# Steps of attention and of the weight sums in other slots, and the sign of converted weights by a sloped ReLU

## The chip, the cores and the metric

The kernel runs on one core of one Trainium2 chip. A core has a matrix engine (TensorE, PE in the profile), a vector engine (VectorE, DVE), a scalar engine (ScalarE, ACT), GpSimd (POOL) and SyncE (SP), which here issues the transfers (DMA). Each engine takes its own instructions in order and waits where an input isn't there yet. The metric is the device time of one execution in microseconds (us).

## What is computed

Chunked attention, then a feed-forward layer with a gated activation, all in float32:

```python
scores = scale * np.matmul(q_c, k_c.transpose(0, 1, 2, 4, 3))      # q, k, v: 8 x 8 heads x 576 x 64, chunks of 64
scores = scores - np.max(scores, axis=-1, keepdims=True)
attn = np.exp(scores)
attn = attn / (np.sum(attn, axis=-1, keepdims=True) + 1e-09)
x = np.matmul(attn, v_c)                                           # reordered to 4608 tokens x 512
h = x @ w_in                                                       # 512 x 2048
g = h * np.clip(h + 3.0, 0.0, 6.0) / 6.0
out = g @ w_out                                                    # 2048 x 512
```

The two weight matrices are handed over as float64 and are converted to float32 on the core.

## The kernel before, in words

The 4608 tokens are nine blocks of 512. Every float32 product is done in three passes (`passes`, L219): each operand is split into a rounded high part and the rest, and TensorE multiplies high by high, high by low and low by high. So VectorE and ScalarE split everything that enters a product: ScalarE makes the high part, VectorE subtracts it.

**Weights.** They come as 16 tiles of 1 MB. `convert` (L100) takes the two 32-bit words of each float64 apart. ScalarE multiplies the high word, read as a float32, by 2^-112 (L106); VectorE shifts the result left by 3 bits (L107), which leaves exponent and mantissa in place and drops the sign; a VectorE instruction takes the sign bit from the high word and puts it in (L108, the mask); ScalarE scales the low word (L110), VectorE adds it (L111), and L115 and L116 split the sum into high and low.

**Blocks 0 to 2** are done directly, by slots. A slot pair is one of the 16 tiles of the hidden dimension: the even slot holds `mm1` (L225, 12 matmuls of 128x512, then ScalarE's Relu L233, VectorE's L234, ScalarE's cast L235 and, at the end of the slot, VectorE's L236, which give the two parts of `g`), the odd slot holds `mm2` (L242, another 12 matmuls, two pairs behind). A slot's 12 matmuls set its length on TensorE. There are 96 slots, in four segments of the blocks 0, 1, 0, 2.

**Blocks 3 to 8** follow in three pairs with a fast scheme of seven products in place of eight (`first_product` L498, `second_product` L558). It needs sums and differences of quarters of the weights, which are made during the slots and kept in DRAM: `prepare(m, p)` (L328) is one unit, sixteen of them. A unit stores three raw quarters (L333, three transfers), adds the two parts of two weight tiles (L337, twice), makes four sums or differences (L347), casts them to high parts in the buffer `hl` (L350, ScalarE), subtracts for the low parts (L352) and stores four quarters from `hl` (L355, four transfers). Both `a` and `hl` have one buffer each.

**Attention** of a block is done in two halves (`Attention`, L128): loads of q and k and of v by SP, scores (64 matmuls, L154), softmax in four steps (maximum L161; subtraction L164 and ScalarE's exponential L165; sum L168 and reciprocal; product L172), transposes on TensorE (L183), ScalarE's copy of them out of PSUM (L185), the matmuls with V (L194), and the copy of the result (L200, or L203 and L206). All its PSUM goes through one buffer of two banks, `two`.

**The order.** Up to slot 30 (`SUMS`) the planner of the framework orders the instructions of each engine by its own costs. From there on the order is that of the program, written out in `plan`: a table from the slot to the steps that follow that slot's own instructions, sorted by a rank. Attention's rank is the place of the step in its list, the unit steps have rank 20, so within a slot attention comes first. Attention of the halves of blocks 2 to 4 starts at slots 30, 38, 52, 60, 68 and 76 (L418), each with the offsets of `later`. The sixteen units start at slots 30, 33, 36, 40, 43, 46, 50, 53, 57, 60, 63, 67, 70, 73, 77 and 80, one step a slot. At slot 86 (`FREE`) the room of the weights and of the sums is given to the fast scheme.

Of the kernel before, what the change touches and what calls it, by code (L numbers as in the profile page):

```python
# [8 lines left out]
F32 = mybir.dt.float32  # L9
# [4 lines left out]
AF = mybir.ActivationFunctionType  # L14
ALU = mybir.AluOpType
# [15 lines left out]
NFP = NFT // 2  # L31
# [10 lines left out]
def tile_kernel(ctx: ExitStack, tc: tile.TileContext, qk_in, v_in, weights, out):  # L42
    nc = tc.nc
    PE, ACT, DVE, POOL = nc.tensor, nc.scalar, nc.vector, nc.gpsimd
# [44 lines left out]
    words, w, w_h, w_l = {}, {}, {}, {}  # L89
# [10 lines left out]
    def convert(ft):  # L100

        u = wsc.tile([P, 1024], I32, name="u")
        r = wsc.tile([P, 1024], I32, name="r")
        lo, hi = words[ft][:, :, 0], words[ft][:, :, 1]

        ACT.activation(out=u.bitcast(F32), in_=hi.bitcast(F32), func=AF.Copy, scale=2.0 ** -112)  # L106
        DVE.tensor_scalar(out=u, in0=u, scalar1=3, scalar2=None, op0=ALU.logical_shift_left)  # L107
        DVE.scalar_tensor_tensor(out=u, in0=hi, scalar=-2 ** 31, in1=u, op0=ALU.bitwise_and, op1=ALU.bitwise_or)  # L108

        ACT.activation(out=r, in_=lo.bitcast(U32), func=AF.Copy, scale=2.0 ** -29)  # L110
        DVE.tensor_tensor(out=u, in0=u, in1=r, op=ALU.add)  # L111
        a = u.bitcast(F32).rearrange("p (m t) -> p m t", m=2)
        w[ft] = w_tile(ft, F32R)
        w_h[ft], w_l[ft] = w[ft][:, 0], w[ft][:, 1]
        ACT.copy(out=w_h[ft], in_=a)  # L115
        DVE.tensor_tensor(out=w_l[ft], in0=a, in1=w_h[ft].bitcast(F32), op=ALU.subtract)  # L116

    def convert_to(ft):
        nonlocal converted
        load_to(ft + 3)  # L120
        while converted < min(ft, NFT):
            convert(converted)
            converted += 1
# [91 lines left out]
    def finish():  # L215
        while low:
            low.pop(0)()
# [56 lines left out]
    def moe_slots(n, ft, *seg):  # L274

        g = mm1(n, ft)
        yield
        pending.append((n, ft, g, *seg))
        if len(pending) > LAG:
            mm2(*pending.pop(0))  # L280
        yield
# [35 lines left out]
    def kept(m, p, i):  # L317

        if m:
            return stream_b[i, p // 4][:, p % 4]  # L320
        k = ORDER_A.index(i)
        return stream_a[p, k // 4][:, k % 4]

    def quarter(m, row, col):

        return (col, row) if m else (row, col)

    def prepare(m, p):  # L328
        cols = lambda k: slice(256 * k, 256 * k + 256)
        for i, row, col in ((1, 0, 0), (2, 0, 1), (4, 1, 1)):  # L330
            f, k = quarter(m, row, col)
            to = kept(m, p, i).rearrange("p (l t) -> p l t", l=2)
            nc.sync.dma_start(out=to, in_=w[p + NFP * f][:, :, m, cols(k)].bitcast(F32))  # L333
        a = sp.tile([P, 2, 512], F32, name="a")
        for f in range(2):
            h, l = [w[p + NFP * f][:, k, m].bitcast(F32) for k in range(2)]
            DVE.tensor_tensor(out=a[:, f], in0=h, in1=l, op=ALU.add)  # L337
        yield

        def q(row, col):  # L340
            f, k = quarter(m, row, col)
            return a[:, f, cols(k)]


        for to, x, y, op in ((q(1, 1), q(1, 0), q(1, 1), ALU.add), (q(1, 0), q(0, 0), q(1, 0), ALU.subtract),
                             (q(0, 0), q(1, 1), q(0, 0), ALU.subtract), (q(0, 1), q(0, 1), q(0, 0), ALU.subtract)):
            DVE.tensor_tensor(out=to, in0=x, in1=y, op=op)  # L347
        hl = sp.tile([P, 2, 2, 2, 256], F32R, name="hl")
        s = a.rearrange("p f (k t) -> p f k t", k=2)
        ACT.copy(out=hl[:, :, :, 0], in_=s)  # L350
        yield
        DVE.tensor_tensor(out=hl[:, :, :, 1], in0=s, in1=hl[:, :, :, 0].bitcast(F32), op=ALU.subtract)  # L352
        for i, row, col in ((5, 1, 1), (7, 1, 0), (6, 0, 0), (3, 0, 1)):
            f, k = quarter(m, row, col)
            nc.sync.dma_start(out=kept(m, p, i), in_=hl[:, f, k].rearrange("p l t -> p (l t)").bitcast(F32))  # L355
        yield


# [4 lines left out]
    def fetch():  # L363
        if stream:
            t, n = stream.pop(0)
            w = wsp.tile([P, 4, 2, 256], F32R, name="ws")
            nc.sync.dma_start(out=w[:, :n].rearrange("p n l t -> p (n l t)").bitcast(F32), in_=t[:, :n].rearrange("p n t -> p (n t)"))
            ahead.append(w)
# [11 lines left out]
    def x_operands(s, eng):  # L380

        n = NSTD + 2 * s
        b = [[xraw[n + j][:, i] for j in range(2)] for i in range(NDP)]
        sub = lambda out, x, y: eng.tensor_tensor(out=out, in0=x, in1=y, op=ALU.subtract)
        ops[s] = {}
        sub(b[0][1], b[0][1], b[0][0])
        for i in ORDER_A:
            ops[s][i] = operand()
            r, c = WHERE[i]
            split(ops[s][i], b[r][c])  # L390

            if i == 5:
                sub(b[0][1], b[1][1], b[0][1])
            elif i == 6:
                sub(b[0][0], b[0][1], b[0][0])
                sub(b[0][1], b[1][0], b[0][1])
            yield
# [3 lines left out]

    plan = {}
    early = [(0, "load_qk"), (1, "load_v"), (2, "scores"), (2, "softmax"), (7, "transpose"), (10, "values")]
    later = [(-2, "load_qk"), (3, "load_v"), (3, "scores"), (4, "soft", 0), (4, "soft", 1), (5, "soft", 2), (5, "soft", 3),
             (8, "transpose"), (9, "values")]

    def put(n, dp, at, steps, stretch=1.0):
        a = Attention(n, dp)
# [7 lines left out]
    SUMS = first[1] + 22  # L416
    FREE = first[3] + 2 * (NFP + LAG + 1)
    for (n, dp), at in zip(((2, 0), (2, 1), (3, 0), (4, 0), (4, 1), (3, 1)), (30, 38, 52, 60, 68, 76)):  # L418
        put(n, dp, at, later)
    for u in range(2 * NFP):  # L420
        for k in range(3):
            plan.setdefault(SUMS + u * (FREE - 2 - SUMS) // (2 * NFP) + k, []).append((20, lambda: next(prep)))
    prep = (step for p in range(NFP) for m in range(2) for step in prepare(m, p))
    slot = 0
    sp = made = None
    order = ExitStack()

    for i, (n, lo, hi) in enumerate(SEGMENTS):
        last = all(m != n for m, *_ in SEGMENTS[i + 1:])
        for ft in range(lo, hi):  # L430
            if i == 0:
                convert_to(min(ft + 2, 4))
            elif slot < SUMS:

                with tc.issue_after(second.done.ins):
                    convert_to(5)
                with tc.issue_after(second.last.ins):
                    convert_to(min(6 + 2 * ft, NFT))
            elif slot == SUMS:
                scratch.close()  # L440
                sums = ExitStack()
                sp = sums.enter_context(tc.tile_pool(name="sp", bufs=1, side="right"))
                op = sums.enter_context(tc.tile_pool(name="op", bufs=4, side="right"))
                order.enter_context(tc.manual_schedule())
            for _ in moe_slots(n, ft, ft == lo, ft == hi - 1, not last):
                for _, f in sorted(plan.pop(slot, []), key=lambda s: s[0]):
                    f()
                finish()
                slot += 1
                if slot == FREE:  # L450
                    assert next(prep, None) is None
                    sums.close()
                    op = None
                    start.close()
                    upper.close()
                    xop_pool = pool("xop", 8, side="right")
                    wsp = pool("wsp", 3, side="right")
                    for _ in range(3):
                        fetch()
                    made = x_operands(0, DVE)  # L460
                elif slot > FREE:
                    next(made, None)
# [197 lines left out]
```

## Time and profile before

| what | value |
|---|---|
| median of 3 runs | 855.14 us (854.91 to 855.72) |
| the profiled execution | 855.06 us |
| its span, first to last instruction | 853.1 us |
| instructions | 13690 |
| transfers | 172.86 MB, mean 203 GB/s |
| mean granted TensorE clock | 0.982 |

The profile is one execution, taken by the hardware. Its page gives each engine's busy time; the views asked of the trace give the groups of instructions by line of the kernel, the waits (who waited for whom, in total, how often, and the longest), the timeline (start, duration, engine, line, operation, tile written and tiles read, and in brackets the idle time of the engine before it and what ended it), and windows (busy time of every engine in a stretch, with the clock that TensorE was granted as a share of full speed). Engines PE and PEld are the matmuls and the weight loads of TensorE; the latter overlap the former, and matmuls overlap one another, so durations of single matmuls don't add up. The stretch from the first matmul of block 0 to about 127 us is ordered by the planner; from 127 to 321 us run the slots 30 to 85; the fast scheme fills the rest.

### The profile page before, as it was taken

What the parts mean: (1) busy time and instruction counts of PE and PEld (TensorE: products, weight loads), DVE (VectorE), ACT (ScalarE), POOL (GpSimd) and SP (SyncE); (2) the same over time, 40 slices, a digit from 0 to 9 for tenths busy, and PEclk for the clock granted to TensorE, in tenths of its full rate; (3) what the DMA queues carried; (4) which work ended last, traced back from release to release, by engine and by line L of the source; (5) the groups of instructions that cost most, each with busy time, mean ns of one, the idle gap of its engine ahead of it and who ended that gap; (6) DMA issues with size and microseconds to landing.
All of it is one profiled execution on the core that took longest, in us unless ns stands there. A gap on an engine that the chain in (4) does not pass through costs nothing.

```text
span 853.1 us, 13690 instructions
## 1 busy us (share of the span) xinstructions
PE 814.5 (95%) x5683; PEld 658.7 (77%) x5683; DVE 635.8 (75%) x768; ACT 369.1 (43%) x455; POOL 132.0 (15%) x77
## 2 busy tenths in 40 slices
PE   7889999789998999999999999999999999999998
PEld 5766878568776777878878888788788887887886
DVE  5978997585866776487699946876899466669951
ACT  4747763243334334334455443344554333336330
POOL 0000000000001000022227002222370022326200
PEclk9898999899999999999999999999999999999999
DMA  9893003856768745166655576666554765555563
GB/s 365 315 360 120 13 0 112 247 184 214 220 187 296 237 160 196 60 232 226 244 189 191 229 254 228 233 214 245 204 192 167 234 226 178 207 186 197 197 212 134
DMA packets 50014, 172.86 MB, mean 203 GB/s; under 512 B 4640, under 2 KB 16928, under 8 KB 39200
## 3 DMA queue, kind: packets, MB, share of 16 engines
q1 hardware_dynamic: 49952, 171.99, 58.0%
q8 instruction: 45, 0.74, 0.3%
q14 instruction: 17, 0.14, 0.1%
HBM read 133.17 MB, written 38.80 MB: 202 GB/s over the span
## 4 chain that ended last, share of the span: by engine, by line
PE 67%; DVE 22%; ACT 5%; issue 3%; DMA 2%; POOL 0%; SPq 0%; ACTq 0%; DVEq 0%
PE acc L221 14%; PE acc L223 14%; PE acc L222 14%; PE h L221 7%; PE h L222 7%; PE h L223 7%; PE two L194 2%; DVE xop L373 2%; DVE m L161 2%; DVE r L234 2%; DVE z L168 1%; DMA w<-w_in_out 1%; DVE a L347 1%; DVE e L164 1%; DVE g L496 1%
## 5 line engine op out<-in xcount | busy, mean ns | idle before, releaser
L221 PE MATMUL acc<-xop,ws 128*128 128x512 f32 x528 | 208.6, 396 | 4.4 <-DVE u L484 4.4
L222 PE MATMUL acc<-xop,ws 128*128 128x512 f32 x528 | 205.8, 390 | 0.0
L223 PE MATMUL acc<-xop,ws 128*128 128x512 f32 x528 | 205.4, 390 | 0.0
L221 PEld LDWEIGHTS acc<-xop,ws 128*128 128x128 f32 x528 | 99.1, 188 | 27.6 <-DVE u L484 6.8
L373 DVE TENSOR_TENSOR xop<-g,xop 128x1024 fp32r<-128x1024 f32 x72 | 103.4, 1468 | 21.5 <-ACT xop L372 21.5
L223 PEld LDWEIGHTS acc<-xop,ws 128*128 128x128 f32 x528 | 99.1, 188 | 20.9
L222 PEld LDWEIGHTS acc<-xop,ws 128*128 128x128 f32 x528 | 99.2, 188 | 19.8
L372 ACT CAST xop<-g 128x1024 fp32r<-128x1024 f32 x72 | 74.4, 1051 | 78.9 <-PE acc L223 51.3
L504 POOL TENSOR_TENSOR g<-g 128x512 f32<-128x512 f32 x24 | 34.8, 1449 | 307.3 <-DVE g L496 307.3
L221 PE MATMUL h<-x,w 128*128 128x512 f32 x192 | 80.0, 419 | 2.1 <-ACT x L203 1.2
L222 PE MATMUL h<-x,w 128*128 128x512 f32 x192 | 78.4, 409 | 0.0
L223 PE MATMUL h<-x,w 128*128 128x512 f32 x192 | 77.8, 405 | 0.0
L222 PE MATMUL acc<-g,w 128*128 128x512 f32 x192 | 75.5, 393 | 0.3 <-DVE g L236 0.3
L221 PE MATMUL acc<-g,w 128*128 128x512 f32 x192 | 75.4, 397 | 0.1
L223 PE MATMUL acc<-g,w 128*128 128x512 f32 x192 | 75.4, 393 | 0.0
L234 DVE SCALAR_TENSOR_TENSOR r<-r,h 128x512 f32<-128x512 f32 x48 | 32.8, 683 | 50.7 <-ACT r L233 50.7
L495 ACT ACTIVATE r<-acc,half 128x512 f32<-128x512 f32 x72 | 48.5, 685 | 26.3 <-DVE acc L484 25.4
L495 ACT ACTIVATE r<-h,half 128x512 f32<-128x512 f32 x24 | 16.5, 687 | 95.0 <-DVE h L484 95.0
L222 PE MATMUL h<-xop,ws 128*128 128x512 f32 x144 | 56.2, 390 | 0.2 <-DVE xop L373 0.2
L221 PE MATMUL h<-xop,ws 128*128 128x512 f32 x144 | 56.3, 391 | 0.0
L223 PE MATMUL h<-xop,ws 128*128 128x512 f32 x144 | 56.1, 389 | 0.0
L496 DVE SCALAR_TENSOR_TENSOR g<-r,acc 128x512 f32<-128x512 f32 x72 | 48.6, 683 | 7.0 <-ACT r L495 6.7
(93 smaller groups left out, 1270.5 us busy)
## 6 DMA issues: line engine op xcount, KB each, us to landing
ws<-b SPq DMA_DIRECT2D x42, 1024.0 KB, 4.8
ws<-a SPq DMA_DIRECT2D x24, 1024.0 KB, 4.9
ws<-a SPq DMA_DIRECT2D x24, 768.0 KB, 4.3
qk<-qk_in SPq DMA_DIRECT2D x17, 1024.0 KB, 6.6
w<-w_in_out SPq DMA_DIRECT2D x16, 1024.0 KB, 13.4
v<-v_in SPq DMA_DIRECT2D x17, 512.0 KB, 5.1
a<-hl SPq DMA_DIRECT2D x32, 256.0 KB, 3.4
b<-hl SPq DMA_DIRECT2D x32, 256.0 KB, 3.4
```

The lines of the kernel that those rows point to most:

```text
L161: DVE.tensor_reduce(out=self.m, in_=flat(self.s), axis=AX.X, op=ALU.max)
L164: DVE.tensor_tensor(out=flat(self.e), in0=flat(self.s), in1=wide(self.m), op=ALU.subtract)
L194: PE.matmul(po[o, s, a, i, :], lhsT=self.v[rows, a, i, o], rhs=self.aT[rows, a, i, o], start=True, stop=True)
L221: PE.matmul(ps, lhsT=a_h, rhs=b_h, start=first, stop=False, skip_group_check=more)
L222: PE.matmul(ps, lhsT=a_h, rhs=b_l, start=False, stop=False, skip_group_check=more)
L223: PE.matmul(ps, lhsT=a_l, rhs=b_h, start=False, stop=last, skip_group_check=more)
L234: DVE.scalar_tensor_tensor(out=r, in0=r, scalar=1.0, in1=h, op0=ALU.min, op1=ALU.mult)
L372: ACT.copy(out=t[:, :, 0], in_=src)
L373: DVE.tensor_tensor(out=t[:, :, 1], in0=src, in1=t[:, :, 0].bitcast(F32), op=ALU.subtract)
L495: return (lambda: ACT.activation(out=r, in_=ps, func=AF.Relu, bias=half, scale=1.0 / 6.0), lambda: DVE.scalar_tensor_tensor(out=out, in0=r ...
L496: lambda: DVE.scalar_tensor_tensor(out=out, in0=r, scalar=1.0, in1=ps, op0=ALU.min, op1=ALU.mult))
L504: sub = lambda o, x, y: lambda: POOL.tensor_tensor(out=o, in0=x, in1=y, op=ALU.subtract)
```

## The change

Two things are changed. In `convert`, ScalarE's scaling uses a ReLU with a slope for negative inputs (Prelu) of 2^32 in place of a copy: positive words are scaled by 2^-112 as before, negative ones by 2^-80, so that their exponent field has one bit more set, and the shift by 3 moves this bit into the sign. The mask on VectorE goes. In the plan, every step of `later` comes one slot sooner, except that v is loaded after the first two steps of softmax, at the same offset as before; and a unit of the weight sums has four steps in place of three: the two additions; the four sums; the cast; the subtraction with the four stores, after which come the three raw stores that stood first. Each unit is now a generator of its own.

```diff
@@ convert
-        ACT.activation(out=u.bitcast(F32), in_=hi.bitcast(F32), func=AF.Copy, scale=2.0 ** -112)
+        ACT.activation(out=u.bitcast(F32), in_=hi.bitcast(F32), func=AF.Prelu, scale=2.0 ** -112, alpha=2.0 ** 32)
         DVE.tensor_scalar(out=u, in0=u, scalar1=3, scalar2=None, op0=ALU.logical_shift_left)
-        DVE.scalar_tensor_tensor(out=u, in0=hi, scalar=-2 ** 31, in1=u, op0=ALU.bitwise_and, op1=ALU.bitwise_or)
@@ prepare
-        for i, row, col in ((1, 0, 0), (2, 0, 1), (4, 1, 1)):
-            f, k = quarter(m, row, col)
-            to = kept(m, p, i).rearrange("p (l t) -> p l t", l=2)
-            nc.sync.dma_start(out=to, in_=w[p + NFP * f][:, :, m, cols(k)].bitcast(F32))
         a = sp.tile([P, 2, 512], F32, name="a")
...
             DVE.tensor_tensor(out=to, in0=x, in1=y, op=op)
+        yield
         hl = sp.tile([P, 2, 2, 2, 256], F32R, name="hl")
...
             nc.sync.dma_start(out=kept(m, p, i), in_=hl[:, f, k].rearrange("p l t -> p (l t)").bitcast(F32))
+        for i, row, col in ((1, 0, 0), (2, 0, 1), (4, 1, 1)):
+            f, k = quarter(m, row, col)
+            to = kept(m, p, i).rearrange("p (l t) -> p l t", l=2)
+            nc.sync.dma_start(out=to, in_=w[p + NFP * f][:, :, m, cols(k)].bitcast(F32))
         yield
@@ plan
-    later = [(-2, "load_qk"), (3, "load_v"), (3, "scores"), (4, "soft", 0), (4, "soft", 1), (5, "soft", 2), (5, "soft", 3),
-             (8, "transpose"), (9, "values")]
+    later = [(-3, "load_qk"), (2, "scores"), (3, "soft", 0), (3, "soft", 1), (3, "load_v"), (4, "soft", 2), (4, "soft", 3),
+             (7, "transpose"), (8, "values")]
...
-        for k in range(3):
-            plan.setdefault(SUMS + u * (FREE - 2 - SUMS) // (2 * NFP) + k, []).append((20, lambda: next(prep)))
-    prep = (step for p in range(NFP) for m in range(2) for step in prepare(m, p))
+        unit = prepare(u % 2, u // 2)
+        for k in range(4):
+            plan.setdefault(SUMS + u * (FREE - 2 - SUMS) // (2 * NFP) + k, []).append((20, lambda unit=unit: next(unit)))
```

More of the change, by code (lines that the diff above doesn't have):

```diff
@@ L450, in tile_kernel @@
                 if slot == FREE:
-                    assert next(prep, None) is None
                     sums.close()
```

## The prediction

> **What bounds the kernel now.** I read the page's busy shares first, then who waited for whom (on TensorE from 127 to 321 us, where blocks 2 to 4 get their attention, and on ScalarE over the whole span; the columns are the total, the number of waits and the longest), then the timeline around each wait, and last the granted clock in windows.
>
> ```profile
> PE 814.5 (95%) x5683; PEld 658.7 (77%) x5683; DVE 635.8 (75%) x768; ACT 369.1 (43%) x455; POOL 132.0 (15%) x77
> ```
>
> ```profile
> PE two L194 <- ACT e L185: 17.1, 6, 6.4
> ```
>
> ```profile
> ACT hl L350 <- DVE a L347: 24.1, 12, 5.3
> ...
> ACT hl L350 <- DMA b<-hl: 5.4, 1, 5.4
> ```
>
> TensorE sets the time; what can be won is where it stands still. In that stretch one line holds all of it, 17.1 us: the matmuls with V (L194) waiting for ScalarE's copy of the transposed weights of attention (L185), six times, once for each `put(..., later)`. The three longest, and the last:
>
> ```profile
> 159.95 1.98 PE L194 MATMUL two<-e,v 64*64 64x64 f32 x64 [6.35 <-ACT e L185]
> ...
> 190.25 1.69 PE L194 MATMUL two<-e,v 64*64 64x64 f32 x64 [2.72 <-ACT e L185]
> ...
> 264.14 1.16 PE L194 MATMUL two<-e,v 64*64 64x64 f32 x64 [2.69 <-ACT e L185]
> ...
> 320.99 1.16 PE L194 MATMUL two<-e,v 64*64 64x64 f32 x64 [2.03 <-ACT e L185]
> ```
>
> The same 64 matmuls take 1.16 us in the last two of these and 1.98 and 1.69 us in the first two: there the clock had dropped. The windows show that (after the window and its length come each engine's busy time, then the granted clock, PEclk):
>
> ```profile
> 61.00:71.20 10.20, 7.87 (x81) 5.96 (x80) 7.48 (x8) 5.61 (x6) 0.00 (x0) 0.50 0.91 363
> 156.50:163.40 6.90, 3.45 (x68) 3.05 (x69) 2.78 (x4) 3.66 (x5) 0.00 (x0) 0.51 0.90 304
> 190.70:194.10 3.40, 3.40 (x56) 2.88 (x46) 2.42 (x5) 1.40 (x2) 0.00 (x0) 0.50 1.07 310
> 265.80:269.20 3.40, 3.40 (x9) 2.63 (x8) 0.82 (x1) 0.58 (x1) 0.00 (x0) 0.50 1.08 387
> 127.00:321.00 194.00, 176.76 (x1414) 142.50 (x1412) 136.97 (x212) 70.94 (x93) 3.11 (x2) 0.96 0.65 206
> ```
>
> The three waits of 6.35, 2.72 and 2.69 us are each followed by half clock in which TensorE worked 3.45, 3.40 and 3.40 us; at full clock that is half the time, so 10.25 / 2 = 5.1 us more is lost. The wait of 2.03 us and the two shorter ones cost none: the three windows' 13.7 us at half clock make a mean of 0.965 over the stretch, which is the row's 0.96. So the six places hold 17.1 + 5.1 = 22.2 us, all in the stretch 127 to 321 us. Its row also shows that neither VectorE (137.0 of 194 us) nor ScalarE (70.9) is full there: what is late is late by order, not by amount.
>
> Why it is late is seen in the timeline at the second one (start, duration, engine; in brackets the idle time before and what ended it):
>
> ```profile
> 180.91 1.23 DVE L172 TENSOR_TENSOR e<-e,z 128x1024 f32<-128x1024 f32 x1
> ...
> 183.26 0.68 DVE L234 SCALAR_TENSOR_TENSOR r<-r,h 128x512 f32<-128x512 f32 x1
> ...
> 183.70 1.04 PE L183 MATMUL two<-ident,e 128*128 128x128 f32 x8
> 183.97 0.62 ACT L235 CAST g<-r 128x512 fp32r<-128x512 f32 x1 [4.95 <-DVE r L234]
> ...
> 185.73 1.05 ACT L350 CAST hl<-a 128x1024 fp32r<-128x1024 f32 x1 [1.14 <-DVE a L347]
> ...
> 187.96 0.68 DVE L234 SCALAR_TENSOR_TENSOR r<-r,h 128x512 f32<-128x512 f32 x1
> ...
> 188.67 0.62 ACT L235 CAST g<-r 128x512 fp32r<-128x512 f32 x1 [1.31 <-DVE r L234]
> ...
> 189.20 1.00 ACT L185 COPY e<-two 128x1024 f32<-128x1024 f32 x1
> ```
>
> The transposes run at 183.70 and V's matmuls could start at 190.25 - 2.72 = 187.53, so the slot of 12 matmuls between them lasts 187.53 - 183.70 - 1.04 = 2.8 us, and the copy has that long. But ScalarE takes its queue in order: ahead of the copy stand the previous slot pair's `g` (waiting for L234, which VectorE reached at 183.26 because softmax and the weight sums were in front of it), the sums' `hl` cast (waiting for L347), and this slot's own Relu and `g`, whose L234 came at 187.96. The copy ends at 190.20.
>
> **The change, part by part.** Durations of the pieces that move:
>
> ```profile
> L347 DVE TENSOR_TENSOR a<-a 128x256 f32<-128x256 f32 x64 | 27.1, 423 | 1.6
> ...
> L337 DVE TENSOR_TENSOR a<-w 128x512 f32<-128x512 f32 x32 | 21.7, 719 | 0.0
> ...
> L352 DVE TENSOR_TENSOR hl<-a,hl 128x1024 fp32r<-128x1024 f32 x16 | 19.5, 1221 | 3.4 <-ACT hl L350 3.4
> ...
> L108 DVE SCALAR_TENSOR_TENSOR u<-w,u 128x1024 int32<-128x1024 int32 x16 | 19.5, 1219 | 0.0
> ...
> L106 ACT ACTIVATE u<-w 128x1024 f32<-128x1024 f32 x16 | 18.5, 1154 | 6.3 <-DMA w<-w_in_out 3.6 <-DVE w L116 2.6
> ...
> L71 ACT ACT_TABLE_LOAD x1 | 1.3, 1283 | 0.7 <-PEq L653 0.7
> ```
>
> and of the stores (KB each, median us from issue to landing):
>
> ```profile
> a<-hl SPq DMA_DIRECT2D x32, 256.0 KB, 3.4
> ...
> a<-w SPq DMA_DIRECT2D x24, 256.0 KB, 5.2
> ```
>
> First, attention moves one slot earlier. All starting slots are even, so the transposes go from an mm1 slot to the mm2 slot before it, V's matmuls to the mm1 slot. An mm2 slot has no Relu and no `g`. Between transposes and copy only the previous mm1 slot's `g` can stand, so two ScalarE operations and one VectorE operation leave the path. Softmax too runs one slot, 2.8 us, sooner. Put into the rows above: the transposes would end at 183.70 - 2.8 + 1.04 = 181.9, the copy is due at 181.9 + 2.8 = 184.7, and the `g` ahead of it ends at 184.6 even if VectorE stays as late as it was; the copy would end at 185.6, 0.9 us late. If softmax's 2.8 us reach L234 as well, `g` ends at about 181.8 and the copy at 182.9, 1.8 us early. So each remaining wait is bounded by 0.0 and 0.9 us; I take 0, since the second follows from the new order, and keep 6 x 0.9 = 5.4 us for the range.
>
> Second, the sums of a unit go from three steps to four. The `hl` cast comes one slot after L347 (four of 0.42, 1.7 us), so ScalarE's 24.1 us of waiting for L347 in front of Relus goes; it was on the path only where it stood ahead of the copy, and that is counted above. VectorE's load per unit is unchanged (two L337, four L347, one L352: 1.4 + 1.7 + 1.2 us); units start 3 or 4 slots apart, so the last step of one and the first of the next often share a slot, after attention's steps. The worst pair, softmax with L352, L337 and L347 over two slots, holds 4.9 of softmax (four passes like L172's) + 4.3 of sums + 1.4 of gating (L234 and its like, L236) = 10.6 us against 5.6 us of TensorE. It was as much before, but the backlog now has one slot more before a copy depends on it.
>
> Third, SP's queue. The three raw quarter stores follow the four `hl` stores of their unit. SP then issues seven in a row; a load of qk or v behind them loses some 1.8 us of issue (the four took 1.8 us, the row 149.37 below). qk is still issued five slots, 14 us, ahead of its scores and v five ahead of its use, so nothing is due. The `hl` buffer is single: its next cast comes two slots after the stores, as before, 5.6 us against 3.4 us to landing. I cost that at nothing; if the cover goes, ScalarE stands as in the 5.4 us row.
>
> ```profile
> 149.37 1.79 SPq L355 DMA_DIRECT2D b<-hl  x4
> ```
>
> Fourth, the mask. 16 x 1.22 = 19.5 us of VectorE work vanish; L106 keeps its shape and operands, only the function changes, so its price is that of its own row (1154 ns). No row shows this function. Most of the 19.5 us lies beside TensorE work: only what delays a TensorE wait counts.
>
> ```profile
> 17.89 1.22 DVE L108 SCALAR_TENSOR_TENSOR u<-w,u 128x1024 int32<-128x1024 int32 x1
> ...
> 21.10 1.21 DVE L172 TENSOR_TENSOR g<-g,z 128x1024 f32<-128x1024 f32 x1
> ...
> 31.45 1.16 PE L154 MATMUL two<-qk 64*64 64x64 f32 x64
> ...
> 34.50 1.22 DVE L161 TENSOR_REDUCE m<-two 128x16 f32<-128x1024 f32 x1
> ...
> 60.79 1.80 PE L183 MATMUL two<-ident,e 128*128 128x128 f32 x8 [2.01 <-DVE e L172]
> ...
> 63.69 1.98 PE L194 MATMUL two<-e,v 64*64 64x64 f32 x64 [1.10 <-ACT e L185]
> ...
> 66.86 0.79 PE L221 MATMUL h<-x,w 128*128 128x512 f32 x1 [1.18 <-ACT x L203]
> ...
> 122.02 1.22 DVE L108 SCALAR_TENSOR_TENSOR u<-w,u 128x1024 int32<-128x1024 int32 x1
> ...
> 123.89 0.50 PE L221 MATMUL h<-x,w 128*128 128x512 f32 x1 [0.77 <-DVE r L234]
> ```
>
> The first mask stands in front of the L172 that the first block's second transposes wait for: 1.1 us (a start-to-start step). Block 1's attention follows in a chain through `m` at 34.50, which came 34.50 - 32.6 = 1.9 us after its scores had ended, behind another three masks. With those gone `m` starts at the scores' end, itself 1.1 us earlier: 3.0 us in all. The chain ends in the 2.01 us wait at 58.8, which then falls to about 0.1. The mask at 122.02 directly delays the L234 of the last row: 0.8 us. Sum 3.8 us. The order there is the planner's, so the bounds are wide: 0 (it reorders and TensorE waits as long) and 3.8 + 3.9 = 7.7 us, where the half clock of 61.0 to 71.2, 7.87 us of work, goes with the wait. I leave that half clock in, since it held through the 1.10 and 1.18 us waits that stay.
>
> The profiled execution took 855.06 us (span 853.1 and 2.0 around it; the median is 855.14): 855.1 - 17.1 - 5.1 - 3.8 = 829.1, so 829.0. The steady stage after 321 us gets none of it back: it loses next to no TensorE time today and nothing in it is edited.
>
> [...]
>
> **The rivals.**
> (a) Half stays: VectorE's peak, moved with softmax, still makes L234 late before the copy, or scores and transposes wait instead. For it: 10.6 us of work in 5.6. Against: a slot more of slack. Time: 829 + 11 = 840.
> (b) The hole at 58.8 to 71 closes as a whole. For: the wait of 2.03 us before 320.99 left the clock full, and masks gone from the whole chain may free more than I count. Time: 829 - 3.9 - 1.1 - 1.2 = 823.
> (c) The sloped ReLU is not in the loaded table. The profile shows one table load, 1283 ns, for Exp, Relu and Copy together; nothing shows the new function; that one table serves three so unlike makes a fourth likely, hence a small chance. At two loads per conversion, ScalarE gets 2.6 us more in each: 5.1 us ahead of the first two weights and, at 66 to 110 us with eight conversions, 20.5 us where 44.0 - 33.1 = 10.9 are free (row below). Time: 829 + 5.1 + 9.6 = 844. [...]
>
> ```profile
> 66.00:110.00 44.00, 42.95 (x172) 33.30 (x173) 41.52 (x48) 33.12 (x40) 0.00 (x0) 0.94 0.12 46
> ```
>
> (d) Slower: the `hl` buffer. If the seven stores share the queue so that the four land later than 5.6 us (the raw ones take 5.2), the next cast blocks ScalarE as at 150.6 to 156.0, and each of the six copies sits behind it. Price: 6 x (6.35 + 1.7) = 48.3 us in place of 22.2, so 855.1 + 26.1 - 3.8 = 877. It makes the kernel slower from 26.0 / 6 = 4.3 us per attention. Against: the four go first, and the copy has one slot more.
> (e) Nothing moves: TensorE waits as long for something else, 855.
>
> **How the numbers follow.** Forecast 0.66, (a) 0.15, (b) 0.10, (c) 0.03, (d) 0.04, (e) 0.02. The range 822 to 842 holds the forecast with its bounds (829.0 + 5.4 + 3.8 = 838.2 above), (a) and (b); (c), (d) and (e) are left out. A difference of 0.2%, 1.7 us, is about what can be told from none. Faster 0.94, same 0.02, slower 0.04.
>
> **What would show it.** Right: no wait of L194 for L185 over 1 us after 127 us; clock 1.00 from 127 to 321; that stretch some 22 us shorter; `hl` waiting for L347 near nothing; VectorE 19.5 us less busy; still one table load, L106 at about 1.15 us. Wrong: a wait over 2 us at those six places, a long `hl` wait for a DMA, or table loads in the conversions.

## The result and the profile after

The changed kernel takes 828.73 us (median of 4 runs, 827.55 to 828.76) against 855.38 us (4 runs, 854.91 to 855.72): a ratio of 0.9685, 95% interval 0.9669 to 0.9702. The prediction was 829.0, in a range of 822 to 842. The total is right to 0.3 us; its terms are not, as three landmarks show. One further run of the kernel before, beside the first four experiments, took 1367.02 us at a mean clock of 0.611; it is left out below, so the median of before beside them is 855.47 us, and the 7.6 us that an expectation names are 7.4. Line numbers move by one to three: the copy of the transposes is now L186, the products with V L195, the cast of the sums L348, the sloped ReLU L108.

From the timeline of TensorE, the first matmul of the fast scheme before, and then the first matmul of slot 30 and of the fast scheme after (the prediction's row at 123.89 is slot 30 before):

```profile
354.87 0.39 PE L221 MATMUL acc<-xop,ws 128*128 128x512 f32 x1
```

```profile
117.00 0.39 PE L222 MATMUL h<-x,w 128*128 128x512 f32 x1
...
328.67 0.39 PE L222 MATMUL acc<-xop,ws 128*128 128x512 f32 x1
```

| stretch | before | after | difference | forecast |
|---|---|---|---|---|
| up to slot 30 | 123.9 | 117.0 | -6.9 | -3.8 |
| slots 30 to 95 and the last products | 231.0 | 211.7 | -19.3 | -22.2 |
| fast scheme | 498.2 | 498.1 | -0.1 | 0 |

Of TensorE's waits from 117 to 300 us, one is left, the sixth of the products with V (the waits, then the timeline):

```profile
PE two L195 <- ACT e L186: 2.3, 1, 2.3
```

```profile
284.60 1.03 PE L184 MATMUL two<-ident,e 128*128 128x128 f32 x8
290.67 1.98 PE L195 MATMUL two<-e,v 64*64 64x64 f32 x64 [2.29 <-ACT e L186]
```

The windows show what is left of half clock, two spells, and the whole stretch from slot 30 to the fast scheme:

```profile
61.80:65.20 3.40, 3.18 (x8) 1.98 (x8) 3.27 (x4) 0.73 (x1) 0.00 (x0) 0.50 1.03 416
290.50:293.90 3.40, 3.23 (x67) 2.92 (x68) 1.84 (x3) 2.34 (x4) 0.00 (x0) 0.50 0.62 216
117.00:328.70 211.70, 209.41 (x1634) 170.84 (x1633) 157.55 (x233) 85.31 (x113) 3.44 (x2) 0.99 0.63 209
```

The groups and the page's first part show the new function's price, the one table load and what the engines do in all:

```profile
PE 806.0 (97%) x5683; PEld 653.0 (79%) x5683; DVE 619.5 (75%) x752; ACT 366.7 (44%) x455; POOL 132.3 (16%) x77
```

```profile
L108 ACT ACTIVATE u<-w 128x1024 f32<-128x1024 f32 x16 | 18.6, 1161 | 3.2 <-DMA w<-w_in_out 3.2
...
L71 ACT ACT_TABLE_LOAD x1 | 1.3, 1283 | 0.7 <-PEq L654 0.7
```

The sloped ReLU costs 1161 ns where the copy cost 1154, and there is still one table load. VectorE has 16 instructions and 16.3 us of busy time less, not the mask's whole 19.5 us. Some 2 us of the difference are overlap: busy time counts once what two neighbouring records share, and the mask's record of 1.22 us was a step of 1.1 us from start to start.

### The profile page after: what moved, and what is told of

It reads as the page before. It is cut to its first block, busy times and chain, and to the rows that moved or that the text cites. A ratio compares the mean times of both kernels' runs of the same rounds, so it can differ in the third digit from the quotient of the medians.

```text
span 826.8 us, 13680 instructions
## 1 busy us (share of the span) xinstructions
PE 806.0 (97%) x5683; PEld 653.0 (79%) x5683; DVE 619.5 (75%) x752; ACT 366.7 (44%) x455; POOL 132.3 (16%) x77
## 4 chain that ended last, share of the span: by engine, by line
PE 80%; DVE 9%; ACT 4%; DMA 3%; issue 2%; SPq 1%; POOL 0%; ACTq 0%; DVEq 0%
PE acc L222 17%; PE acc L224 16%; PE acc L223 16%; PE h L223 9%; PE h L224 9%; PE h L222 8%; DMA w<-w_in_out 3%; PE two L195 2%; DVE xop L375 2%; PE two L155 1%; DVE g L497 1%; PE two L184 1%; DVE u L485 1%; ACT r L496 1%; DVE g L552 1%
## 5 line engine op out<-in xcount | busy, mean ns | idle before, releaser
L222 PE MATMUL h<-x,w 128*128 128x512 f32 x192 | 76.8, 401 | 3.3 <-ACT x L204 2.5
L223 PE MATMUL h<-x,w 128*128 128x512 f32 x192 | 76.4, 398 | 0.2 <-DVE x L207 0.2
L224 PE MATMUL h<-x,w 128*128 128x512 f32 x192 | 76.0, 396 | 0.1
L496 ACT ACTIVATE r<-h,half 128x512 f32<-128x512 f32 x24 | 16.5, 687 | 94.4 <-DVE h L485 94.4
L234 ACT ACTIVATE r<-h,half 128x512 f32<-128x512 f32 x48 | 33.1, 690 | 49.7 <-PE h L224 49.6
```

The source lines that it names most:

```text
L222: PE.matmul(ps, lhsT=a_h, rhs=b_h, start=first, stop=False, skip_group_check=more)
L223: PE.matmul(ps, lhsT=a_h, rhs=b_l, start=False, stop=False, skip_group_check=more)
L224: PE.matmul(ps, lhsT=a_l, rhs=b_h, start=False, stop=last, skip_group_check=more)
L234: ACT.activation(out=r, in_=h, func=AF.Relu, bias=half, scale=1.0 / 6.0)
L496: return (lambda: ACT.activation(out=r, in_=ps, func=AF.Relu, bias=half, scale=1.0 / 6.0), lambda: DVE.scalar_tensor_tensor(out=out, in0=r ...
```

## The experiments

**Each edit by itself.** Four kernels ran on the same chip beside the kernel before (855.47 us). The first is the changed kernel with the old conversion:

```diff
-        ACT.activation(out=u.bitcast(F32), in_=hi.bitcast(F32), func=AF.Prelu, scale=2.0 ** -112, alpha=2.0 ** 32)
+        ACT.activation(out=u.bitcast(F32), in_=hi.bitcast(F32), func=AF.Copy, scale=2.0 ** -112)
         DVE.tensor_scalar(out=u, in0=u, scalar1=3, scalar2=None, op0=ALU.logical_shift_left)
+        DVE.scalar_tensor_tensor(out=u, in0=hi, scalar=-2 ** 31, in1=u, op0=ALU.bitwise_and, op1=ALU.bitwise_or)
```

> Both plan edits, with the conversion as before (mask kept). Theory 1 (the two halves of the change act in separate stretches and add up): the start of slot 30 stays where it was before, near 123.9 us, the stretch behind it is 19.3 us shorter, so about 836. Theory 2 (the plan also needs VectorE ahead of time, that is the mask gone): some of the six waits come back, 840 to 846.

835.35 us, ratio 0.9761 (0.9746 to 0.9775): -20.1 us. Theory 1 holds: the plan needs nothing from the sign. The one wait of 2.28 us at the sixth place stands here as well, but in this execution no half clock followed it (mean clock 0.990; the other three runs have 0.988).

The second is the reverse, the kernel before with only these lines of `convert` changed.

> The sloped ReLU without the mask, with the plan as before. Theory 1: about 855.4 - 6.9 = 848.5, with the two stretches of half clock before 72 us gone or shorter, and the six waits of the V matmuls in blocks 2 to 4 still some 17 us. Theory 2 (only the VectorE time on the path counts, no clock): 855.4 - 3.8 = 851.6.

848.09 us, 0.9915 (0.9898 to 0.9931): -7.4 us. Theory 1 holds, and the waits of the products with V are the old ones:

```profile
PE two L193 <- ACT e L184: 16.9, 6, 6.1
```

Sign and plan thus act in separate stretches and add up, to about 1 us: 20.1 + 7.4 = 27.5 against 855.38 - 828.73 = 26.7 us.

The third and the fourth take the plan apart, on the kernel before: only the offsets of attention,

```diff
-    later = [(-2, "load_qk"), (3, "load_v"), (3, "scores"), (4, "soft", 0), (4, "soft", 1), (5, "soft", 2), (5, "soft", 3),
-             (8, "transpose"), (9, "values")]
+    later = [(-3, "load_qk"), (2, "scores"), (3, "soft", 0), (3, "soft", 1), (3, "load_v"), (4, "soft", 2), (4, "soft", 3),
+             (7, "transpose"), (8, "values")]
```

> Only the list of attention's offsets is changed; sums in three steps and the mask as before. Theory 1 (one slot's distance is what takes the waits away): 836 to 840, at most two of the six waits above 1 us. Theory 2 (the cast of the sums that stood in ScalarE's queue waiting for VectorE was the cause): four or more waits stay, 846 to 852.

and only `prepare` in four steps with the raw stores last.

> Only the weight sums are changed: four steps, raw stores behind; attention and the mask as before. Theory 1: ScalarE's wait of the cast for the four sums falls from 24 us to under 10, but the copy still stands behind Relu and cast of its own slot: 848 to 853. Theory 2 (the cast was the cause): 836 to 842.

Attention alone: 841.16 us, 0.9831 (0.9816 to 0.9846), -14.3 us. The sums alone: 858.14 us, 1.0029 (1.0017 to 1.0041), 2.7 us slower. Theory 1 holds for the first, just outside its range. For the second both theories are wrong about the time, theory 2 by far. From TensorE's waits in slots 30 to 95, attention alone:

```profile
PE two L194 <- ACT e L185: 5.5, 3, 4.3
```

What is left there has the cast in it. With attention moved and the sums in three steps, the cast stands directly ahead of the copy at the second, third and fifth place, and the longest wait, 4.28 us at the fifth, has the cast waiting as long for its buffer (ScalarE's timeline):

```profile
274.62 1.04 ACT L350 CAST hl<-a 128x1024 fp32r<-128x1024 f32 x1 [4.28 <-DMA a<-hl]
275.57 1.01 ACT L185 COPY e<-two 128x1024 f32<-128x1024 f32 x1
```

The sums alone, TensorE's and then ScalarE's waits, and ScalarE's timeline at the fifth place:

```profile
PE two L194 <- ACT e L185: 16.5, 6, 4.3
```

```profile
ACT hl L347 <- DMA a<-hl: 5.6, 2, 3.4
...
ACT hl L347 <- DVE a L343: 3.6, 4, 1.1
```

```profile
283.50 0.62 ACT L235 CAST g<-r 128x512 fp32r<-128x512 f32 x1 [4.58 <-DVE r L234]
287.51 1.04 ACT L347 CAST hl<-a 128x1024 fp32r<-128x1024 f32 x1 [3.39 <-DMA a<-hl]
288.46 0.68 ACT L233 ACTIVATE r<-h,half 128x512 f32<-128x512 f32 x1
289.90 0.62 ACT L235 CAST g<-r 128x512 fp32r<-128x512 f32 x1 [0.76 <-DVE r L234]
290.43 1.01 ACT L185 COPY e<-two 128x1024 f32<-128x1024 f32 x1
```

The cast's wait for VectorE fell from 24.1 to 3.6 us, and TensorE got nothing for it: 16.5 us of waits in place of 17.1. Moved by a slot, the cast stands ahead of other copies, and here it waits for its single buffer, whose stores were late because VectorE was: L349, which they follow, ran at 280.32, behind softmax's second half. Only with attention moved as well is the fourth step worth something: 20.1 us together against 14.3 - 2.7 = 11.6 us for the two single gains. The parts of the plan don't add up, since each of them decides which copies the cast stands ahead of; with both, it is the sixth alone.

**Which move of attention.** Two kernels keep all of the change but one half of attention's shift: transposes and product with V at the old offsets, or scores and softmax at the old ones. They and the next two ran beside 855.81 us.

```diff
-             (7, "transpose"), (8, "values")]
+             (8, "transpose"), (9, "values")]
```

> The changed kernel with transposes and the product with V back at their old offsets (8 and 9), softmax and all else as changed. Theory 1 (the copy must not stand behind the Relu and cast of its own slot): at least three of the six waits come back with 0.5 us or more, 832 to 840. Theory 2 (one slot more between softmax and the transposes is what counts, wherever it comes from): no wait above 0.5 us but the last, 827 to 829.

837.88 us, 0.979 (0.9766 to 0.9815). Theory 1: all six waits come back, though there is a slot more between softmax and the transposes than there was before. At the first and fourth place, where no cast of the sums stands directly ahead of the slot's Relu, `g` and copy, they are 1.11 and 1.25 us; the three longest, 2.1 to 3.1 us, have it there.

```diff
-    later = [(-3, "load_qk"), (2, "scores"), (3, "soft", 0), (3, "soft", 1), (3, "load_v"), (4, "soft", 2), (4, "soft", 3),
+    later = [(-3, "load_qk"), (3, "scores"), (3, "load_v"), (4, "soft", 0), (4, "soft", 1), (5, "soft", 2), (5, "soft", 3),
```

> The changed kernel with scores and softmax back at their old offsets (3, 4 and 5), transposes and the product with V at the new ones (7 and 8). Theory 1 (place of the copy in the queue): each wait stays at 0.9 us or less on average, the sum at most 5.4 us, 829 to 835. Theory 2 (distance from softmax): TensorE waits as long as in the kernel before, 16 us or more with the clock, 840 to 848.

833.24 us, 0.9737 (0.9723 to 0.9752). Theory 1 again: with softmax as late as before, the place of the copy alone keeps its waits small. Now the transposes wait for softmax. TensorE's waits of the two kernels, early softmax first:

```profile
PE two L195 <- ACT e L186: 11.1, 6, 3.1
```

```profile
PE two L184 <- DVE e L173: 4.2, 4, 1.7
PE two L195 <- ACT e L186: 1.5, 2, 0.9
```

**The order of the stores.**

```diff
+        for i, row, col in ((1, 0, 0), (2, 0, 1), (4, 1, 1)):
+            ...
         for i, row, col in ((5, 1, 1), (7, 1, 0), (6, 0, 0), (3, 0, 1)):
             ...
-        for i, row, col in ((1, 0, 0), (2, 0, 1), (4, 1, 1)):
-            ...
```

> The changed kernel with the three raw stores ahead of the four stores from the cast's buffer in the last step of a unit. Theory 1 (the transfers have cover: the buffer's next cast comes two slots later): ScalarE's waits of the cast for a DMA stay under 12 us in total (6 now), none of them reaches a copy but the last, 828 to 830. Theory 2 (the stores decide when the buffer is free): 10 us more of such waits at the six copies, 833 or more.

830.90 us, 0.9705 (0.9689 to 0.9721), between the two theories. The cast waits 14.0 us for transfers (6.0 in the changed kernel), and TensorE now waits at three places, 4.0 us in all:

```profile
ACT hl L348 <- DMA b<-hl: 8.5, 3, 5.2
...
ACT hl L348 <- DMA a<-hl: 5.5, 3, 2.8
```

The time is some 2 us above the changed kernel's, which was measured on another chip, and the intervals overlap: the order of the stores is worth little in time, if anything, though the cast's waits for its buffer more than double.

**The wait that stayed.** At the sixth place of the changed kernel the timeline of VectorE, then of ScalarE, reads:

```profile
278.56 0.69 DVE L235 SCALAR_TENSOR_TENSOR r<-r,h 128x512 f32<-128x512 f32 x1 [2.71 <-ACT r L234]
...
282.04 1.22 DVE L350 TENSOR_TENSOR hl<-a,hl 128x1024 fp32r<-128x1024 f32 x1
283.30 1.29 DVE L334 TENSOR_TENSOR a<-w 128x512 f32<-128x512 f32 x2
...
285.11 1.80 DVE L344 TENSOR_TENSOR a<-a 128x256 f32<-128x256 f32 x4
286.82 0.68 DVE L235 SCALAR_TENSOR_TENSOR r<-r,h 128x512 f32<-128x512 f32 x1
```

```profile
287.54 0.62 ACT L236 CAST g<-r 128x512 fp32r<-128x512 f32 x1 [4.78 <-DVE r L235]
288.66 1.04 ACT L348 CAST hl<-a 128x1024 fp32r<-128x1024 f32 x1 [0.50 <-DMA a<-hl]
289.61 1.00 ACT L186 COPY e<-two 128x1024 f32<-128x1024 f32 x1
```

Only here do softmax's second half, one unit's L350 and the next unit's L334 meet in one slot (80), with L344 in the next: VectorE runs from 278.56 to 287.5 without a pause, so `g` of slot 82 is late, and the last unit's cast, in the same slot 82, stands between `g` and the copy. The rows give each its size: V's matmuls could start at 290.67 - 2.29 = 288.38; right behind `g` the copy would have ended at about 289.1, so some 0.8 us belong to the late `g` and 1.5 us to the cast with its wait. One slot's delay of that unit takes both away:

```diff
-            plan.setdefault(SUMS + u * (FREE - 2 - SUMS) // (2 * NFP) + k, []).append((20, lambda unit=unit: next(unit)))
+            plan.setdefault(SUMS + u * (FREE - 2 - SUMS) // (2 * NFP) + (u == 15) + k, []).append((20, lambda unit=unit: next(unit)))
```

> The changed kernel with the sixteenth unit of the sums one slot later (slot 81 in place of 80), so that slot 80 loses one pair of additions, and the cast of the last unit falls into the slot of the transposes, behind the copy. Theory 1 (the one wait that is left, 2.29 us at 288.4, comes from what stands ahead of the copy in ScalarE's and VectorE's queues): the wait falls under 0.5 us and the half clock behind it goes, 824.7 to 826.5. Theory 2 (ScalarE's exponential and the fourteenth unit's cast ahead of the Relu of slot 80 hold it up): the wait stays at 1.5 us or more, 828 to 829.

824.71 us, 0.9635 (0.9621 to 0.9649). Theory 1 holds, and this version beats both kernels; TensorE has no wait for the copy left in these slots. The run doesn't separate the cast from the late `g`. Its ScalarE queue at that place:

```profile
285.44 0.63 ACT L236 CAST g<-r 128x512 fp32r<-128x512 f32 x1 [2.94 <-DVE r L235]
285.97 1.00 ACT L186 COPY e<-two 128x1024 f32<-128x1024 f32 x1
288.44 1.04 ACT L348 CAST hl<-a 128x1024 fp32r<-128x1024 f32 x1 [1.47 <-DMA a<-hl]
```

The cast now waits even longer for its buffer, behind the copy, where it costs nothing.

**What the half clock costs.** Idle matmuls fill the wait that stayed; the rest is the changed kernel.

```diff
+    plan[84].append((7.5, lambda: warm_up(20)))
```

> The changed kernel with 20 idle matmuls of 128x256 (bfloat16, results unused) on TensorE just ahead of the sixth product with V, where TensorE waited 2.29 us and the clock halved behind it. Theory 1 (the halving comes from the wait and costs half of the 3.4 us that follow): the copy ends as late as before, the half clock at 290 us is gone, 828.7 - 1.7 = 827.0. Theory 2 (the halving costs nothing, or has another cause): 828.5 to 829.

827.96 us, 0.9676 (0.9664 to 0.9688), beside 855.04 us. In the profile the matmuls lie in the wait, and the window after it has the full clock:

```profile
289.05 2.36 PE L81 MATMUL h<-ident 128*128 128x256 bf16 x20
291.55 0.64 PE L195 MATMUL two<-e,v 64*64 64x64 f32 x28
```

```profile
287.00:296.00 9.00, 8.86 (x109) 7.18 (x108) 4.59 (x7) 4.70 (x6) 0.00 (x0) 1.00 0.81 256
```

So the idle time of the wait caused the halving, as far as one profile of each kernel shows. The price isn't settled by the medians: 0.8 us apart, with intervals that overlap. In the profiled executions the end lies 826.3 - 62.46 = 763.8 us behind the first product of block 1 here and 826.8 - 61.54 = 765.3 us in the changed kernel, 1.5 us, close to the 1.7 expected; this execution had lost 0.9 us ahead of that point. From slot 30 to the fast scheme it is 211.7 us in the changed kernel, 210.3 here and 210.4 in the plan alone, where no half clock followed the same wait: 1.2 to 1.4 us.

**Where the sign's gain comes from.** The kernel before with the sloped ReLU for some tiles only (beside 855.04 us): `ft < 4` chooses it in the first kernel, `ft >= 4` in the second, and the others keep copy and mask.

```diff
+        if ft < 4:
+            ACT.activation(out=u.bitcast(F32), in_=hi.bitcast(F32), func=AF.Prelu, scale=2.0 ** -112, alpha=2.0 ** 32)
+        else:
             ACT.activation(out=u.bitcast(F32), in_=hi.bitcast(F32), func=AF.Copy, scale=2.0 ** -112)
...
+        if ft >= 4:
             DVE.scalar_tensor_tensor(out=u, in0=hi, scalar=-2 ** 31, in1=u, op0=ALU.bitwise_and, op1=ALU.bitwise_or)
```

> The kernel before with the sloped ReLU for the first four of the sixteen weight tiles only; the other twelve keep the mask. Theory 1 (the gain of the sign comes from the chain of block 1's attention, which the first four masks delay): 5 to 6.5 us of the 7.6, 849 to 851. Theory 2 (it comes from VectorE being nearly full from 66 to 127 us): at most 3 us, 852.5 or more.

> The reverse: the sloped ReLU for the last twelve tiles, the mask for the first four. Theory 1: only the 0.8 us wait at 123 us goes and perhaps a little of the late start, 854 to 855. Theory 2: 4 us or more, 851 or less.

850.57 us, 0.9948 (0.9935 to 0.9960), and 856.53 us, 1.0007 (0.9998 to 1.0017). Theory 1 holds in the main: four masks of sixteen bring 4.5 us, a little less than it said, and twelve bring nothing that can be told from none (their median lies above theory 1's range), though VectorE was 94% busy from 66 to 110 us while most of them ran. All sixteen brought 7.4. The profiles place these gains (all sixteen is the kernel with the sign alone):

| us | before | first four | last twelve | all sixteen |
|---|---|---|---|---|
| block 1 starts | 66.9 | 62.3 | 68.1 | 61.5 |
| from there to slot 30 | 57.0 | 56.8 | 55.7 | 55.4 |

The last twelve do shorten the second stretch by 1.3 us, as theory 2 had it, but in that kernel block 1 starts 1.3 us later and takes it back. Between the first four and all sixteen lie 0.8 us ahead of block 1's start and 1.5 us behind it.

## Why the prediction was right, and where not

**Order, not amount.** Shown, for the waits. The late copy in ScalarE's queue was the cause: with the copy moved ahead of its slot's Relu and cast, the waits go even where softmax stays late (1.5 us of them left), and with softmax early but the copy in its old place they come back (11.1 us).

**"Each remaining wait is bounded by 0.0 and 0.9 us; I take 0."** Right for five of six, wrong for the sixth, which waited 2.29 us. The bound was worked out at the second place and carried to the others. It took the previous `g` for the only thing that can stand ahead of the copy. A late `g` alone cost 0.8 us at the sixth place, inside the bound; the cast of the sums, which stands there too, put 1.5 us on top. By the prediction's own sign, a wait over 2 us at one of the six places, its mechanism was wrong there. The prediction did name the worst pair of slots (10.6 us of work in 5.6), but didn't ask at which of the six places it falls.

**The clock term.** 5.1 us were to go. Half clock where TensorE worked fell from 10.25 to 3.23 us in this stretch, so 3.5 us went; the rest came behind the wait that stayed. Of the stretch's 19.3 us the rows carry 17.1 - 2.3 = 14.8 us of waits and 3.5 us of clock; 1.0 us I can't place. At the six places before, half clock came behind the waits of 2.69 us and more and not behind that of 2.03 us. Here it came behind 2.29 us, and with the idle matmuls in that place the granted clock stayed at 1.00 (287 to 296 us). The length of a wait alone doesn't tell: 2.28 us in the plan alone cost no clock (last section). That the three waits of before cost 5.1 us was a figure of one execution.

**The sums' steps "counted above", the stores "at nothing".** The total was right, the parts weren't looked at. By themselves the four steps make the kernel 2.7 us slower, and with attention moved they bring 20.1 - 14.3 = 5.8 us. The cast's wait for the additions was to be near nothing; 8.1 us stayed, in two waits of 4.0, at 138 and 231 us, and no wait of TensorE follows them. That the transfers have cover holds for the order chosen; with the raw stores first, the waits for the buffer more than double.

**The mask, 3.8 us.** The step that failed is the mis-sized chain: 6.9 us came. Its rows after:

```profile
31.37 0.29 PE L155 MATMUL two<-qk 64*64 64x64 f32 x4
...
32.84 1.22 DVE L162 TENSOR_REDUCE m<-two 128x16 f32<-128x1024 f32 x1
...
54.91 1.22 DVE L173 TENSOR_TENSOR e<-e,z 128x1024 f32<-128x1024 f32 x1
...
58.58 0.33 PE L195 MATMUL two<-e,v 64*64 64x64 f32 x6 [1.10 <-ACT e L186]
61.54 0.61 PE L222 MATMUL h<-x,w 128*128 128x512 f32 x1 [1.79 <-ACT x L204]
```

The 1.1 us of the first mask did not carry on (scores at 31.37, before at 31.45, though a spell of half clock from 23.4 to 30.2 us is gone as well), and `m` came 1.7 us sooner, not 3.0. But the planner, with VectorE shorter, also drew the later steps together: the transposes run at 56.45 without a wait (before 60.79, 4.3 us) and block 1 starts at 61.54 (before 66.86, 5.3 us). And the half clock that I left in, 61.0 to 71.2, shrank to 61.8 to 65.2: 7.87 us of half-rate work became 3.18, worth 2.3 us of the 6.9. The 1.6 us that come behind block 1's start are mostly half clock and the wait of 0.77 us ahead of slot 30, which is gone as predicted. An order made by a planner is not moved by an edit, it is made anew, and a chain of 30 us of it is no sum of old rows.

**The rivals.** Half of the waits staying (a) and the buffer (d) did not happen, but both have their trace: the sixth wait is in part (a) at one place, and the cast that waits 3.39 us ahead of a copy, with the sums alone, is (d) at one place. The hole of (b) closed in part: half clock shorter, 1.10 and 1.79 us of waiting left. The other table (c) is out: one load, 1283 ns, with the sloped ReLU as with the copy. (e) is out: TensorE's waits fell from 17.1 to 2.3 us.

The total came out to 0.3 us because 3.1 us too little early and 2.9 us too much later cancelled, which is luck, not because the terms were that good.

## What to carry to other kernels

Where an engine takes its queue in order, list for each result that a bottleneck waits for what stands ahead of it in that queue, and do it at every place of a schedule, since units with another period meet each place differently. Two edits of one schedule have to be tried together and apart: the four steps alone cost 2.7 us, and beside the other edit they gained 5.8. Work taken from a busy engine pays only where its results are waited for: four of sixteen masks gave more than half (4.5 of 7.4 us), twelve by themselves nothing in total.

## What had not been expected of the hardware

The same kernel meets half clock differently from one execution to the next. The kernel with twelve sloped ReLUs ran twelve times: four at a mean clock of 0.981 or 0.982 took 854.22 to 854.83 us, the other eight 856.29 to 857.21 us, seven of them at 0.979 or less, the slowest at 0.982. The changed kernel's fourth run had 0.998 where the others had 0.996, and took 1.2 us less. And the same wait of 2.3 us at the sixth place was followed by half clock in the changed kernel's profile and not in that of the plan alone. Within each of the two executions of before and after the spells keep a grid: before, four of them start at 61.0, 156.5, 190.7 and 265.8 us, and the distances of 95.5, 34.2 and 75.1 us are 28, 10 and 22 times 3.41 us, the length of the shortest spell; after, the two of the windows above start at 61.77 and 290.46 us, 67 times 3.41 us apart. Whether another execution of the same kernel has its grid elsewhere isn't shown, with one profile of each kernel.

On the grid the two waits of 2.3 us differ. The changed kernel's stretch of 3.41 us before the spell, then the two stretches of the plan alone that hold its wait:

```profile
287.05:290.46 3.41, 1.33 (x6) 0.76 (x5) 1.87 (x3) 2.42 (x3) 0.00 (x0) 1.00 0.83 240
```

```profile
293.45:296.86 3.41, 2.13 (x10) 1.43 (x8) 1.91 (x4) 1.63 (x3) 0.00 (x0) 1.00 1.04 313
296.86:300.28 3.42, 2.42 (x70) 2.14 (x71) 2.39 (x3) 2.67 (x5) 0.00 (x0) 1.00 0.42 148
```

In the first, TensorE is idle for 3.41 - 1.33 = 2.1 us of one stretch, and half clock follows; in the second, the wait is cut by a grid point into 1.3 and 1.0 us, and none follows. In the profiles of before and after, from slot 30 to the fast scheme, the stretches of the grid at full clock with 2.94, 2.72 and 1.79 us of idle time (before, from 153.12, 187.25 and 262.35 us) and with 2.08 us (after, the row above) were followed by half clock; all others had 1.48 us or less and were followed by full clock. In the first 70 us it isn't as clear: 2.46 and 2.01 us (before) and 2.01 us (after) were followed by half clock, 1.86 us (after, from 13.98 us) by full. So in these executions two waits of 2.3 us had a different price, and the one that a grid point cut in two cost no clock. That the cut is the reason is an estimate of mine from these rows. A difference of 1 to 2 us between two versions of this kernel therefore has to be read with their clocks beside it.
